# Denominators of a linear attention: chunk sums on VectorE, and an LN1 shared by two engines

## The chip, the cores and the metric

The kernel runs on one core of one Trainium2 chip. The metric is the device time of one execution in microseconds. Before the change it is 263.28 us, the median of three runs (262.45 to 264.20). A core has TensorE (PE, matmuls, with its weight loads listed as PEld), VectorE (DVE), ScalarE (ACT), GpSimd (POOL) and SyncE (SP). Each takes its instructions in the order of the program and waits for the others by semaphores. In this kernel nearly all DMAs are issued from SP's queue, which is in order as well: a DMA whose data isn't ready holds back every later one.

## The reference

```python
# x: 2048 x 640; H = 32 heads of 20; F = 1728; all bf16
g = sigmoid((x * gate_w).sum(-1, keepdims=True))

q, k, v = split(x @ wqkv)                 # (32, 2048, 20) each
phi = lambda t: where(t > 0, t + 1, exp(t)) + 1e-6
pq, pk = phi(q), phi(k)
kv  = einsum("bhsd,bhse->bhde", pk, v)
z   = einsum("bhsd->bhd", pk)             # sum of phi(k) over the rows
num = einsum("bhqd,bhde->bhqe", pq, kv)
den = einsum("bhqd,bhd->bhq", pq, z) + 1e-6
a = (num / den) @ wo

h  = gelu(layernorm(x) @ w1)              # LN1
hs = shift_rows_by_quarter(h) @ w2        # quarters of the columns moved by +1, -1, +2, -2 rows
x1 = x + hs
b  = x1 + gelu(layernorm(x1) @ w3) @ w4   # LN2
return g * a + (1 - g) * b
```

## The kernel before, in words

The 2048 rows are 16 chunks of 128 (`c`), in four tiles of 512 (`t`); `cc` is a chunk within its tile. The 640 columns are five blocks of 128 (`j`, `dc`, `fc`). The program order is written out by hand (`manual_schedule`), so the order of the source is the order of each engine's queue.

The stages, with the lines of the profile:

- **k** (L186): 16 chunks of phi(k) into `pk`, rows on partitions. **q** (L241): phi(q) into `pqT`, columns on partitions, so that `pqT[:, j, s]` holds block j of row s. `xT`, the transposed x, is read only up to here.
- **G** (`g_unit(j)`, L318): the product of phi(k) with x, five units of 32 matmuls, each about 4.4 us. x has a column of ones behind it, so column 320 of the second half of each PSUM result is z, the sum of phi(k), for the 128 columns of block j. ScalarE copies the rest to `gs` (L320), two buffers in turn, and SP transposes it into `gT` (L322). VectorE makes `zbd[:, j, :]` (L321), z spread over 32 heads by a mask, as bf16.
- **LN1**: `ln1_stat(c)` takes mean and variance on VectorE (L292 to L294), `ln1_rstd(t)` the reciprocal root for a tile's four chunks on GpSimd (L288, L289), `ln1_apply(c)` writes the normalised chunk on VectorE (L308) and SP transposes it into `lnxT` (L310). These run beside G.
- **w1** (`w1_unit(t, fcs)`, L352): three units for each tile, of two, two and one column blocks. ScalarE applies gelu (L356), and for the last unit writes `hx` (L359), which VectorE copies in four strips into `hsT` (L362).
- **kv** (`kv_unit`, L371): gT with the v weights; VectorE masks the result into `kvT` in three pieces (L377). Then `m_unit(g)` (L385), six units of two matmuls, multiplies with the output weights; ScalarE copies each result to `mst` (L387), `m_store` writes these to DRAM in three DMAs (L391) and `m_load` reads them back, arranged anew, as `m_sb` in six (L397).
- **Denominators**: `den_mm` (L256) multiplies all five blocks of `pqT` with `zbd`, 20 matmuls; the four row tiles go to the four 32-partition strips of one PSUM bank. `den_evac` (L262) adds 1e-6 on VectorE, `den_recip` (L267) takes the reciprocal, `r_spread` copies it to four tiles (L271) and four DMAs spread it over the partitions as `rb` (L273). `scale_t(t)` (L277) multiplies `pqT` of tile t by it.
- **w2** (`w2_unit(t, cc)`, L435) and the residual add into a float32 `x1` tile (L438), then LN2 (`ln2_rstd`, `ln2_apply`, with a transpose from SP at L454). Then for each tile t: **w3** (`w3_unit`, L485, gelu at L487), **att** (`att_unit`, L466, added at L472), **w4** (L524, L560), output.

PSUM results take turns in four pairs of banks (`pair()`): a unit can start only when the result four units earlier has been read out.

What matters for the order around the change: after `g_unit(4)` come `w1_unit(0, ...)` three times, `kv_unit`, `w1_unit(1, (0, 1))`, `den_mm`, three `m_unit`s, `w1_unit(1, (2, 3))`, two `m_unit`s, `w1_unit(1, (4,))`, the last `m_unit`, `m_store`, and `w2_unit(0, ...)`. VectorE does `den_evac`, four `ln1_apply` and `den_recip` in that stretch. `r_spread` follows the last `ln2_apply` of tile 0, and `m_load` follows all of `w1_unit(2, ...)`. In the loop over t, tile 0's w3 units alternate with `w2_unit(1, ...)`, from the first on.

Of the kernel before, what the change touches and what calls it, by code (L numbers as in the profile page):

```python
# [16 lines left out]
def kernel(  # L17
# [32 lines left out]
    NG = 6  # L50
# [11 lines left out]
    small = ctx.enter_context(tc.tile_pool(name="small", bufs=4))  # L62
    work = ctx.enter_context(tc.tile_pool(name="work", bufs=4))
    hx_p = ctx.enter_context(tc.tile_pool(name="hx_p", bufs=3))
    outp = ctx.enter_context(tc.tile_pool(name="outp", bufs=4))
    lnx_p = ctx.enter_context(tc.tile_pool(name="lnx_p", bufs=3))
    ps = ctx.enter_context(tc.tile_pool(name="ps", bufs=4, space=PSUM))
    dram = ctx.enter_context(tc.tile_pool(name="dram", bufs=1, space=bass.MemoryType.DRAM))
# [14 lines left out]
    m_sb = const.tile([P, DC, D], BF16)  # L83
    kvT = const.tile([P, D], BF16)
    rb = const.tile([P, NT, TS], BF16)
    r_bf = const.tile([P, TS], BF16)
    r4 = const.tile([H, NT, TS], BF16)
    ident = const.tile([P, P], BF16)
# [1 line left out]
    g5z = const.tile([P, P], BF16)  # L90
    mhalf = const.tile([P, CPT], F32)
    hmask = const.tile([P, H], F32)
    zbd = const.tile([P, DC, H], BF16)
    bmask = const.tile([P, GH * 4], F32)
    bmask5 = const.tile([P, 8], F32)
    ylog = const.tile([P, NCH], F32)
# [58 lines left out]
    for c in range(0, NCH, CPT):  # L155
# [89 lines left out]
    def gate_ops():  # L245
# [3 lines left out]
        nc.vector.reciprocal(omg[:], omg[:])  # L249
        nc.vector.tensor_tensor(gate[:], gate[:], omg[:], op=ALU.mult)  # L250

    def den_mm():
        pt = pair()
        for j in range(DC):
            for t in range(NT):
                nc.tensor.matmul(pt[32 * t:32 * (t + 1), 0, :], lhsT=zbd[:, j, :], rhs=pqT[:, j, t * TS:(t + 1) * TS],  # L256
                                 start=(j == 0), stop=(j == DC - 1))
        return pt

    def den_evac(pt):  # L260
        d = x1p.tile([P, D], F32, name="x1")[:, 0:TS]
        nc.vector.tensor_scalar_add(d, pt[:, 0, :], 1e-6)  # L262
        return d

    def den_recip(d):
        with nc.allow_low_precision(reason="rounded after a float32 division, as a copy would"):
            nc.vector.reciprocal(r_bf[:], d)  # L267
# [28 lines left out]
    def ln1_stat(c):  # L296
        ln_stats(mv1[:, c, :], x_sb[:, c, 0:D], st1s[:, c])

    def ln1_rstd(t):
        tt = slice(t * CPT, (t + 1) * CPT)  # L300
        rsqrt(rstd1[:, tt], mv1[:, tt, 1])

    def ln1_apply(c):
        t, cc = divmod(c, CPT)
        if cc == 0:
            lnxT[t] = lnx_p.tile([P, DC, TS], BF16, name="lnxT")
        lnx = work.tile([P, D], BF16, name="ln")
        nc.vector.tensor_scalar(lnx[:], x_sb[:, c, 0:D], mv1[:, c, 0:1], rstd1[:, c:c + 1],  # L308
                                op0=ALU.subtract, op1=ALU.mult)
        nc.sync.dma_start_transpose(lnxT[t][:, :, cc * P:(cc + 1) * P], lnx[:])  # L310


    def g_unit(j):
        pt = pair()
        for c in range(NCH):
            w = pk[:, c, :].rearrange("p (m j) -> p j m", j=DC)[:, j]
            for hf in range(2):
                nc.tensor.matmul(pt[:, hf, 0:HD + hf], lhsT=w, rhs=x_sb[:, c, hf * HD:(hf + 1) * HD + hf],  # L318
                                 start=(c == 0), stop=(c == NCH - 1))
        nc.scalar.copy(gs[:, j % 2, :].rearrange("p (h e) -> p h e", h=2), pt[:, :, 0:HD])  # L320
        nc.vector.tensor_scalar_mul(zbd[:, j, :], hmask[:], pt[:, 1, HD:HD + 1])  # L321
        nc.sync.dma_start_transpose(gT[:, :, j * P:(j + 1) * P], gs[:, j % 2, :])  # L322

    for c in range(CPT):
        ln1_stat(c)
    ln1_rstd(0)
    g_unit(0)
    for cc in range(CPT):
        ln1_stat(CPT + cc)
        ln1_apply(cc)  # L330
    ln1_rstd(1)
    g_unit(1)
    for cc in range(CPT):
        ln1_stat(2 * CPT + cc)
        ln1_apply(CPT + cc)
    ln1_rstd(2)
    g_unit(2)
    for cc in range(CPT):
        ln1_stat(3 * CPT + cc)
    ln1_rstd(3)  # L340
    g_unit(3)
    g_unit(4)
    for cc in range(CPT):
        ln1_apply(2 * CPT + cc)


# [35 lines left out]
    def m_unit(g):  # L382
        pt = pair()
        for hf in range(2):
            nc.tensor.matmul(pt[:, hf, 0:HD], lhsT=kvT[:, row0[g]:row0[g] + P],  # L385
                             rhs=wo_sb[:, g, hf * HD:(hf + 1) * HD], start=True, stop=True)
        nc.scalar.copy(mst[g // 2][:, g % 2, :].rearrange("p (h e) -> p h e", h=2), pt[:, :, 0:HD])  # L387

    def m_store():
        for i in range(NG // 2):  # L390
            nc.sync.dma_start(m_dram[2 * i:2 * i + 2].rearrange("g p e -> p g e"), mst[i])  # L391
# [9 lines left out]
    nc.gpsimd.memset(hsT[:, :, S:S + 4], 0.0)  # L401
    for fcs in w1_split:
        w1_unit(0, fcs)
    kv_unit()
    w1_unit(1, w1_split[0])
    s1.close()
    w4p = ctx.enter_context(tc.tile_pool(name="w4p", bufs=1))
    w4_sb = w4p.tile([P, FF + 1, D], BF16)
    h2x_p = ctx.enter_context(tc.tile_pool(name="h2x_p", bufs=2))
    h2p = ctx.enter_context(tc.tile_pool(name="h2p", bufs=1))  # L410
    x1p = ctx.enter_context(tc.tile_pool(name="x1p", bufs=11))
    den = den_evac(den_mm())
    mst = [x1p.tile([P, D], F32, name="x1")[:].bitcast(BF16).rearrange("p (g e) -> p g e", g=2) for _ in range(NG // 2)]
    for cc in range(CPT):
        ln1_apply(3 * CPT + cc)
    den_recip(den)
    for g in range(3):
        m_unit(g)
    w1_unit(1, w1_split[1])
    for g in range(3, 5):  # L420
        m_unit(g)
    w1_unit(1, w1_split[2])
    m_unit(5)
    m_store()
    st = {}


# [104 lines left out]

    def w4_turned_out(t, cc):
        c = t * CPT + cc
        oc = outp.tile([P, D], BF16, name="oc")
        o = t * TS + cc * P
        nc.vector.scalar_tensor_tensor(oc[:].rearrange("p (d f) -> p d f", d=DC), pqT[:, :, o:o + P], omg[:, c:c + 1],  # L537
                                       st[t]["x1"][cc][:].rearrange("p (d f) -> p d f", d=DC), op0=ALU.mult, op1=ALU.add)
        nc.sync.dma_start(out2[c * P:(c + 1) * P, :], oc[:])

    def w4_stt(t, cc, oc, src, a, b):
        c = t * CPT + cc
# [7 lines left out]
    def w4_last(t):  # L550
        pts, ocs = {}, {}

        def place(pairs, homes):
            for cc, (w, n) in homes.items():
                pts[cc, 0], pts[cc, 1] = (pairs[n][:, 1, 0:NW], 0, NW), (pairs[w][:, 0, :], NW, D)

        def mm(cc, hf, start):
            dst, a, b = pts[cc, hf]
            for fc in range(FF):
                nc.tensor.matmul(dst, lhsT=st[t]["h2"][:, fc * TS + cc * P:fc * TS + (cc + 1) * P],  # L560
                                 rhs=w4_sb[:, fc, a:b], start=start and fc == 0, stop=not start and fc == FF - 1)

        prs = [pair() for _ in range(3)]
        place(prs, {0: (0, 1), 2: (1, 2)})
        for cc in (0, 2):
            for hf in (1, 0):
                mm(cc, hf, True)
        prs.append(pair())
        place(prs, {1: (3, 3), 3: (2, 0)})
        for u in range(2):  # L570
            for hf in range(2):
                for v in range(2):
                    rows = slice(FR * v, FR * (v + 1))
                    dst, a, b = pts[u + 2 * v, hf]
                    cc = u + 2 * v
                    nc.tensor.matmul(dst, lhsT=st[t]["h2x"][rows, cc * P:(cc + 1) * P],
                                     rhs=w4_sb[rows, FF, a:b], start=u == 1, stop=u == 0)
        for cc in (0, 2):
            oc = outp.tile([P, D], BF16, name="oc")
            for hf in range(2):  # L580
                w4_stt(t, cc, oc, *pts[cc, hf])
            w4_store(t, cc, oc, 0, D)
        for cc, hf in ((1, 1), (3, 1), (1, 0), (3, 0)):
            mm(cc, hf, False)
            if hf == 1:
                ocs[cc] = outp.tile([P, D], BF16, name="oc")
            w4_stt(t, cc, ocs[cc], *pts[cc, hf])
            w4_store(t, cc, ocs[cc], *pts[cc, hf][1:])

    for cc in range(CPT):  # L590
        w2_unit(0, cc)
        ln2_rstd(0, cc, cc + 1)
        if cc >= 1:
            ln2_apply(0, cc - 1)
    for fcs in w1_split:
        w1_unit(2, fcs)
        if fcs[0] == 0:
            ln2_apply(0, CPT - 1)
            r_spread()
    m_load()  # L600
    nc.sync.dma_start(w4_sb[:, 0:FF, :], B_w4[0:FF * P, :].rearrange("(c p) f -> p c f", p=P))
    nc.sync.dma_start(w4_sb[0:FR, FF, :], B_w4[FF * P:F, :])
    nc.sync.dma_start(w4_sb[FR:P, FF, :], B_w4[FF * P:F, :])
# [57 lines left out]
```

## Time and profile before

| | us |
|---|---|
| median of three runs | 263.28 |
| profiled execution | 262.68 |
| its span, first to last instruction | 261.0 |
| TensorE busy in it | 256.0 |
| VectorE busy | 141.4 |
| ScalarE busy | 93.5 |

The profile page gives totals for each engine, the chain of work that ended last (followed back from the last instruction through whatever released each step), and groups of equal instructions with their mean duration. In a group line the name before the arrow is what is written, those behind it what is read; then the shape, the type, the count, the busy time, the mean in ns and the idle time in front of them with what ended it. Some of the groups around the change:

```profile
L256 PE MATMUL pp<-pqT,zbd 128*32 128x512 bf16 x20 | 1.3, 381 | 0.0
L321 DVE TENSOR_SCALAR zbd<-hmask,pp 128x32 bf16<-128x32 f32 x5 | 1.1, 224 | 1.3 <-ACT gs L320 1.3
L308 DVE TENSOR_SCALAR ln<-x_sb,mv,rstd 128x640 bf16<-128x640 bf16 x16 | 6.3, 424 | 0.4 <-POOL rstd L289 0.3
L320 ACT CAST gs<-pp 128x640 bf16<-128x640 f32 x5 | 3.5, 692 | 19.7 <-PE pp L318 14.4 <-DMA wk_sb<-gs 5.3
L267 DVE RECIPROCAL r_bf<-x 128x512 bf16<-128x512 f32 x1 | 3.3, 3348 | 0.0
```

A matmul's own duration (381 ns here) is longer than its share of the chain, since matmuls overlap in the array.

### The profile page before, as it was taken

What the parts mean: (1) busy time and instruction counts of PE and PEld (TensorE: products, weight loads), DVE (VectorE), ACT (ScalarE), POOL (GpSimd) and SP (SyncE); (2) the same over time, 40 slices, a digit from 0 to 9 for tenths busy, and PEclk for the clock granted to TensorE, in tenths of its full rate; (3) what the DMA queues carried; (4) which work ended last, traced back from release to release, by engine and by line L of the source; (5) the groups of instructions that cost most, each with busy time, mean ns of one, the idle gap of its engine ahead of it and who ended that gap; (6) DMA issues with size and microseconds to landing.
All of it is one profiled execution on the core that took longest, in us unless ns stands there. A gap on an engine that the chain in (4) does not pass through costs nothing.

```text
span 261.0 us, 4113 instructions
## 1 busy us (share of the span) xinstructions
PE 256.0 (98%) x1601; PEld 151.5 (58%) x1625; DVE 141.4 (54%) x276; ACT 93.5 (36%) x144; POOL 27.9 (11%) x82
## 2 busy tenths in 40 slices
PE   8999999999999999999999999999999999999995
PEld 4677555688854644566464566455565546465543
DVE  2688778799947894876300398600287610125132
ACT  1655454321165446532343322342322344342100
POOL 3000050012220140131000131000023000000000
PEclk9999999999999999999999999999999999999999
DMA  7999996016684836994032123312123402211011
GB/s 206 204 147 378 365 338 242 0 28 121 122 107 82 216 65 133 186 311 88 14 43 40 20 52 90 81 23 57 23 50 73 102 20 43 43 44 54 24 50 53
DMA packets 57558, 28.28 MB, mean 108 GB/s; under 512 B 45506, under 2 KB 56770, under 8 KB 57538
## 3 DMA queue, kind: packets, MB, share of 16 engines
q1 hardware_dynamic: 57096, 27.52, 44.1%
q10 hardware_dynamic: 442, 0.49, 0.5%
q8 instruction: 13, 0.21, 0.4%
q14 instruction: 7, 0.06, 0.1%
HBM read 13.03 MB, written 3.60 MB: 64 GB/s over the span
## 4 chain that ended last, share of the span: by engine, by line
PE 98%; issue 1%; DVE 0%
PE pp L485 21%; PE pp L524 16%; PE pp L186 9%; PE pp L318 8%; PE pp L435 8%; PE pp L466 8%; PE pp L241 8%; PE pp L352 8%; PE pp L560 5%; PE pp L199 1%; PE pp L495 1%; PE pp L516 1%; PE pp L385 1%; PE pp L371 1%; PE pp L256 0%
## 5 line engine op out<-in xcount | busy, mean ns | idle before, releaser
L485 PE MATMUL pp<-lnxT,w_sb 128*128 128x512 bf16 x249 | 59.8, 379 | 0.6
L487 ACT ACTIVATE h<-pp 128x1024 bf16<-128x1024 f32 (+1 forms) x28 | 26.9, 962 | 56.0 <-PE pp L485 56.0
L524 PE MATMUL pp<-h,w_sb 128*128 128x512 bf16 (+1 forms) x228 | 42.4, 343 | 0.3
L485 PEld LDWEIGHTS <-w_sb 128*128 128x128 bf16 x260 | 25.2, 98 | 26.9
L438 DVE TENSOR_TENSOR x<-pp,x_sb 128x640 f32<-128x640 f32 x16 | 13.1, 817 | 42.7 <-PE pp L435 42.7
L524 PEld LDWEIGHTS <-w_sb 128*128 128x128 bf16 x234 | 22.7, 98 | 19.5 <-issue 1.0
L178 ACT ACTIVATE e<-pp 128x640 bf16<-128x640 f32 (+1 forms) x26 | 21.5, 827 | 9.5 <-PE pp L241 9.5
L466 PE MATMUL pp<-m_sb,pqT 128*128 128x320 bf16 x160 | 24.3, 299 | 0.0
L472 DVE SCALAR_TENSOR_TENSOR x<-pp,gate,x 128x640 f32<-128x640 f32 x16 | 14.1, 883 | 18.3 <-PE pp L466 12.6
L435 PE MATMUL pp<-w_sb,hsT 128*128 128x320 bf16 x160 | 23.9, 299 | 0.0
L186 PE MATMUL pp<-wk_sb,xT 128*128 128x320 bf16 (+1 forms) x160 | 23.0, 303 | 0.1
L288 POOL TENSOR_SCALAR rstd<-mv 128x1 f32<-128x1 f32 (+1 forms) x20 | 7.7, 385 | 142.1 <-DVE mv L294 142.1
L318 PE MATMUL pp<-x_sb,pk 128*128 128x320 bf16 (+1 forms) x160 | 22.0, 300 | 0.0
L241 PE MATMUL pp<-xT,hsT 128*128 128x512 bf16 x98 | 21.6, 379 | 0.1
L318 PEld LDWEIGHTS <-pk 128*128 128x128 bf16 x160 | 18.8, 117 | 3.2
L435 PEld LDWEIGHTS <-hsT 128*128 128x128 bf16 x160 | 15.6, 98 | 8.0
L466 PEld LDWEIGHTS <-pqT 128*128 128x128 bf16 x160 | 15.7, 98 | 7.7
L537 DVE SCALAR_TENSOR_TENSOR oc<-pqT,omg,x 128x640 bf16<-128x640 bf16 x12 | 10.5, 877 | 16.8 <-DMA pqT<-hx 16.8
L186 PEld LDWEIGHTS <-xT 128*128 128x128 bf16 x160 | 15.6, 99 | 6.9 <-DVE xT L215 0.9
L352 PE MATMUL pp<-lnxT,w_sb 128*128 128x512 bf16 x77 | 17.9, 379 | 0.2
L241 PEld LDWEIGHTS <-hsT 128*128 128x128 bf16 x100 | 11.8, 118 | 9.7
L528 ACT CAST hx<-pp 128x512 bf16<-128x512 f32 x12 | 7.0, 586 | 22.5 <-PE pp L524 14.9
(80 smaller groups left out, 236.6 us busy)
## 6 DMA issues: line engine op xcount, KB each, us to landing
x_sb<-in_A_x_dram SPq DMA_DIRECT2D x1, 2240.0 KB
out_dram<-oc SPq DMA_DIRECT2D x14, 160.0 KB, 1.9
w_sb<-in_B_w_dram SPq DMA_DIRECT2D x1, 2160.0 KB, 11.0
w_sb<-in_B_w_dram SPq DMA_DIRECT2D x1, 2080.0 KB
wo_sb<-in_A_wo_dram SPq DMA_DIRECT2D x6, 160.0 KB, 7.9
m_dram<-x SPq DMA_DIRECT2D x3, 320.0 KB, 5.0
hsT<-in_A_wqkv_dram SPq DMA_DIRECT2D x1, 800.0 KB
m_sb<-in_A_wqkv_dram SPq DMA_DIRECT2D x1, 800.0 KB
```

The lines of the kernel that those rows point to most:

```text
L178: nc.scalar.activation(ev, src, ACT.Exp)
L186: nc.tensor.matmul(pt[:, hf, 0:n], lhsT=xT[:, dc, c * P:(c + 1) * P], rhs=wk_sb[:, dc, hf * HD:hf * HD + n], start=(dc == first), stop=(dc ...
L241: nc.tensor.matmul(pt[:, t % 2, :], lhsT=wq_sb[:, dc, :].rearrange("p (m j) -> p j m", j=DC)[:, j], rhs=xT[:, dc, t * TS:(t + 1) * TS], st ...
L318: nc.tensor.matmul(pt[:, hf, 0:HD + hf], lhsT=w, rhs=x_sb[:, c, hf * HD:(hf + 1) * HD + hf], start=(c == 0), stop=(c == NCH - 1))
L352: nc.tensor.matmul(pt[:, i, :], lhsT=w, rhs=lnxT[t][:, dc, :], start=(dc == 0), stop=(dc == DC - 1))
L435: nc.tensor.matmul(pt[:, hf, 0:HD], lhsT=hsT[:, fc, 2 + c * P:2 + (c + 1) * P], rhs=w2_sb[:, fc, hf * HD:(hf + 1) * HD], start=(fc == 0), ...
L438: nc.vector.tensor_tensor(x1[:].rearrange("p (h e) -> p h e", h=2), pt[:, :, 0:HD], x_sb[:, c, 0:D].rearrange("p (h e) -> p h e", h=2), op ...
L466: nc.tensor.matmul(pt[:, hf, 0:HD], lhsT=pqT[:, j, c * P:(c + 1) * P], rhs=m_sb[:, j, hf * HD:(hf + 1) * HD], start=(j == 0), stop=(j == D ...
L472: nc.vector.scalar_tensor_tensor(x1, pt[:, :, 0:HD], gate[:, c:c + 1], x1, op0=ALU.mult, op1=ALU.add)
L485: nc.tensor.matmul(pt[:, k, :], lhsT=w3_sb[:, dc, fc * P:(fc + 1) * P], rhs=lnT[:, dc, :], start=(dc == 0), stop=(dc == DC - 1))
L487: nc.scalar.activation(h2[:, 2 * i * TS:(2 * i + n) * TS], pt[:].rearrange("p h e -> p (h e)")[:, 0:n * TS], ACT.Gelu_apprx_tanh)
L524: nc.tensor.matmul(dst, lhsT=w4_sb[:, fc, d * P:(d + 1) * P], rhs=st[t]["h2"][:, fc * TS + a:fc * TS + b], start=False, stop=(fc == FF - 1))
```

## The change

z is no longer spread over heads. ScalarE copies it to a float32 `z[:, j]`. `den_add(j)` then sums the five blocks before any matmul: `u = sum over j of z_j * pqT_j`, 128 partitions by 2048 columns in float32, in two halves of 1024 columns. Block 0 is written by ScalarE, the other four are accumulated by VectorE. `u` lies in the memory of `xT`. `den_hi` copies u to bf16 on ScalarE, `den_lo` takes what that rounding lost, also as bf16, on VectorE, and `den_mm` multiplies both parts with the constant head mask: eight matmuls instead of 20.

LN1: of the 16 `ln1_apply`, 12 go to ScalarE (which needs `nmr1`, minus mean times rstd, a small VectorE product); chunks 10 to 13 stay on VectorE. Reciprocal roots of the first and last tile are taken in halves. The last tile's statistics are moved behind G, and its chunks 14 and 15 are applied after `den_evac`. As every gs transpose is issued from the same queue as the LN1 transposes, their order changes too: the last G transpose no longer stands behind as many of them.

In the stage after kv, `den_mm` moves behind the fifth `m_unit`; `den_recip` and `r_spread` move behind the last `ln2_apply` of tile 0, and `m_load` between that tile's first and second `ln2_apply`. The output tiles `oc4` are four fixed ones, and `mst` borrows them and `rb`.

```diff
+    mst = [oc4[:, 0:2, :], oc4[:, 2:4, :], rb[:].rearrange("p t s -> p (t s)")[:, 0:2 * D].rearrange("p (g e) -> p g e", g=2)]
...
-    zbd = const.tile([P, DC, H], BF16)
+    z = const.tile([P, DC], F32)
+    hm_bf = const.tile([P, H], BF16)
...
+    nc.gpsimd.tensor_copy(hm_bf[:], hmask[:])
...
+    halves = (slice(0, S // 2), slice(S // 2, S))
+    u = xT[:, 0:2, :].bitcast(F32).rearrange("p a s -> p (a s)")
+
+    def den_add(j):
+        for sl in halves:
+            if j == 0:
+                nc.scalar.activation(u[:, sl], pqT[:, j, sl], ACT.Copy, scale=z[:, j:j + 1])
+            else:
+                nc.vector.scalar_tensor_tensor(u[:, sl], pqT[:, j, sl], z[:, j:j + 1], u[:, sl], op0=ALU.mult, op1=ALU.add)
+
+    def den_hi(sl):
+        nc.scalar.copy(xT[:, 4, sl], u[:, sl])
+
+    def den_lo(sl):
+        nc.vector.tensor_tensor(xT[:, 3, sl], u[:, sl], xT[:, 4, sl], op=ALU.subtract)
+
     def den_mm():
         pt = pair()
-        for j in range(DC):
+        for n in range(2):
             for t in range(NT):
-                nc.tensor.matmul(pt[32 * t:32 * (t + 1), 0, :], lhsT=zbd[:, j, :], rhs=pqT[:, j, t * TS:(t + 1) * TS],
-                                 start=(j == 0), stop=(j == DC - 1))
+                nc.tensor.matmul(pt[32 * t:32 * (t + 1), 0, :], lhsT=hm_bf[:], rhs=xT[:, 4 - n, t * TS:(t + 1) * TS],
+                                 start=(n == 0), stop=(n == 1))
         return pt
...
+    def ln1_nmr(t, a=0, b=CPT):
+        tt = slice(t * CPT + a, t * CPT + b)
+        nc.vector.scalar_tensor_tensor(nmr1[:, tt], mv1[:, tt, 0], -1.0, rstd1[:, tt], op0=ALU.mult, op1=ALU.mult)
...
+        if eng is nc.scalar:
+            nc.scalar.activation(lnx[:], x_sb[:, c, 0:D], ACT.Identity, bias=nmr1[:, c:c + 1], scale=rstd1[:, c:c + 1])
...
+        nc.scalar.copy(z[:, j:j + 1], pt[:, 1, HD:HD + 1])
         nc.scalar.copy(gs[:, j % 2, :].rearrange("p (h e) -> p h e", h=2), pt[:, :, 0:HD])
-        nc.vector.tensor_scalar_mul(zbd[:, j, :], hmask[:], pt[:, 1, HD:HD + 1])
```

The order beside and behind G in the new kernel (loops written short):

```python
ln1_stat(0..3), rstd after 1 and after 3;  ln1_nmr(0, 0, 2)
g_unit(0);  den_add(0);  ln1_apply(0, 1) on ScalarE
g_unit(1);  ln1_stat(4..7), ln1_nmr(0, 2, 4) after 5;  ln1_rstd(1);  ln1_apply(2, 3) on ScalarE;  den_add(1)
g_unit(2);  ln1_stat(8..11), ln1_nmr(1) after 8;  ln1_rstd(2);  ln1_apply(4..7) on ScalarE
g_unit(3);  den_add(2);  den_add(3);  ln1_nmr(2)
g_unit(4);  den_add(4);  ln1_apply(8, 9) on ScalarE;  ln1_stat(12, 13);  ln1_rstd(3, 0, 2);  ln1_apply(10, 11)
w1_unit(0, ...) x3;  den_hi x2;  kv_unit;  den_lo x2
ln1_stat(14, 15);  ln1_rstd(3, 2, 4);  ln1_apply(12, 13);  w1_unit(1, (0, 1))
m_unit(0), (1);  w1_unit(1, (2, 3));  m_unit(2), (3);  w1_unit(1, (4,));  m_unit(4);  den_mm;  m_unit(5);  m_store
den_evac;  ln1_nmr(3, 2, 4);  ln1_apply(14, 15) on ScalarE
w2_unit(0, 0..3) with ln2_rstd and ln2_apply(0, cc - 1);  m_load after ln2_apply(0, 0)
w1_unit(2, (0, 1));  ln2_apply(0, 3);  den_recip;  r_spread;  w1_unit(2, (2, 3)), (4,)
```

More of the change, by code (lines that the diff above doesn't have):

```diff
@@ L64 @@
     hx_p = ctx.enter_context(tc.tile_pool(name="hx_p", bufs=3))
-    outp = ctx.enter_context(tc.tile_pool(name="outp", bufs=4))
     lnx_p = ctx.enter_context(tc.tile_pool(name="lnx_p", bufs=3))
@@ L85 @@
     rb = const.tile([P, NT, TS], BF16)
+    oc4 = const.tile([P, CPT, D], BF16)
+    mst = [oc4[:, 0:2, :], oc4[:, 2:4, :], rb[:].rearrange("p t s -> p (t s)")[:, 0:2 * D].rearrange("p (g e) -> p g e", g=2)]
     r_bf = const.tile([P, TS], BF16)
@@ L101 @@
     rstd1 = const.tile([P, NCH], F32)
+    nmr1 = const.tile([P, NCH], F32)
     wq_sb = hsT[:, :, 0:D]
@@ L297, in ln1_stat, with ln1_rstd, ln1_apply @@
         ln_stats(mv1[:, c, :], x_sb[:, c, 0:D], st1s[:, c])
-    def ln1_rstd(t):
-        tt = slice(t * CPT, (t + 1) * CPT)
+    def ln1_rstd(t, a=0, b=CPT):
+        tt = slice(t * CPT + a, t * CPT + b)
         rsqrt(rstd1[:, tt], mv1[:, tt, 1])
-    def ln1_apply(c):
+    def ln1_nmr(t, a=0, b=CPT):
+        tt = slice(t * CPT + a, t * CPT + b)
+        nc.vector.scalar_tensor_tensor(nmr1[:, tt], mv1[:, tt, 0], -1.0, rstd1[:, tt], op0=ALU.mult, op1=ALU.mult)
+    def ln1_apply(c, eng=nc.vector):
         t, cc = divmod(c, CPT)
@@ L307, in ln1_apply @@
         lnx = work.tile([P, D], BF16, name="ln")
-        nc.vector.tensor_scalar(lnx[:], x_sb[:, c, 0:D], mv1[:, c, 0:1], rstd1[:, c:c + 1],
-                                op0=ALU.subtract, op1=ALU.mult)
+        if eng is nc.scalar:
+            nc.scalar.activation(lnx[:], x_sb[:, c, 0:D], ACT.Identity, bias=nmr1[:, c:c + 1], scale=rstd1[:, c:c + 1])
+        else:
+            nc.vector.tensor_scalar(lnx[:], x_sb[:, c, 0:D], mv1[:, c, 0:1], rstd1[:, c:c + 1],
+                                    op0=ALU.subtract, op1=ALU.mult)
         nc.sync.dma_start_transpose(lnxT[t][:, :, cc * P:(cc + 1) * P], lnx[:])
@@ L325 @@
         ln1_stat(c)
-    ln1_rstd(0)
+        if c % 2 == 1:
+            ln1_rstd(0, c - 1, c + 1)
+    ln1_nmr(0, 0, 2)
     g_unit(0)
+    den_add(0)
+    for cc in range(2):
+        ln1_apply(cc, nc.scalar)
+    g_unit(1)
     for cc in range(CPT):
         ln1_stat(CPT + cc)
-        ln1_apply(cc)
+        if cc == 1:
+            ln1_nmr(0, 2, CPT)
     ln1_rstd(1)
-    g_unit(1)
+    for cc in range(2, CPT):
+        ln1_apply(cc, nc.scalar)
+    den_add(1)
+    g_unit(2)
     for cc in range(CPT):
         ln1_stat(2 * CPT + cc)
-        ln1_apply(CPT + cc)
+        if cc == 0:
+            ln1_nmr(1)
     ln1_rstd(2)
-    g_unit(2)
     for cc in range(CPT):
+        ln1_apply(CPT + cc, nc.scalar)
+    g_unit(3)
+    den_add(2)
+    den_add(3)
+    ln1_nmr(2)
+    g_unit(4)
+    den_add(4)
+    for cc in range(2):
+        ln1_apply(2 * CPT + cc, nc.scalar)
+    for cc in range(2):
         ln1_stat(3 * CPT + cc)
[L340 to L343, printed above, removed]
+    ln1_rstd(3, 0, 2)
+    for cc in range(2, CPT):
         ln1_apply(2 * CPT + cc)
@@ L403 @@
         w1_unit(0, fcs)
+    for sl in halves:
+        den_hi(sl)
     kv_unit()
-    w1_unit(1, w1_split[0])
+    for sl in halves:
+        den_lo(sl)
+    for cc in range(2, CPT):
+        ln1_stat(3 * CPT + cc)
+    ln1_rstd(3, 2, CPT)
+    for cc in range(2):
+        ln1_apply(3 * CPT + cc)
+    w1_unit(1, w1_split[0])
+    for g in range(2):
+        m_unit(g)
+    w1_unit(1, w1_split[1])
+    for g in range(2, 4):
+        m_unit(g)
+    w1_unit(1, w1_split[2])
+    m_unit(4)
+    den_ps = den_mm()
+    m_unit(5)
+    m_store()
     s1.close()
@@ L411 @@
     x1p = ctx.enter_context(tc.tile_pool(name="x1p", bufs=11))
[L412 to L424, printed above, removed]
+    den = den_evac(den_ps)
+    ln1_nmr(3, 2, CPT)
+    for cc in range(2, CPT):
+        ln1_apply(3 * CPT + cc, nc.scalar)
     st = {}
@@ L534, in w4_turned_out @@
         c = t * CPT + cc
-        oc = outp.tile([P, D], BF16, name="oc")
+        oc = oc4[:, cc, :]
         o = t * TS + cc * P
-        nc.vector.scalar_tensor_tensor(oc[:].rearrange("p (d f) -> p d f", d=DC), pqT[:, :, o:o + P], omg[:, c:c + 1],
+        nc.vector.scalar_tensor_tensor(oc.rearrange("p (d f) -> p d f", d=DC), pqT[:, :, o:o + P], omg[:, c:c + 1],
                                        st[t]["x1"][cc][:].rearrange("p (d f) -> p d f", d=DC), op0=ALU.mult, op1=ALU.add)
-        nc.sync.dma_start(out2[c * P:(c + 1) * P, :], oc[:])
+        nc.sync.dma_start(out2[c * P:(c + 1) * P, :], oc)
     def w4_stt(t, cc, oc, src, a, b):
@@ L578, in w4_last @@
         for cc in (0, 2):
-            oc = outp.tile([P, D], BF16, name="oc")
+            oc = oc4[:, cc, :]
             for hf in range(2):
@@ L585, in w4_last @@
             if hf == 1:
-                ocs[cc] = outp.tile([P, D], BF16, name="oc")
+                ocs[cc] = oc4[:, cc, :]
             w4_stt(t, cc, ocs[cc], *pts[cc, hf])
@@ L594 @@
             ln2_apply(0, cc - 1)
-    for fcs in w1_split:
+        if cc == 1:
+            m_load()
+    w1_unit(2, w1_split[0])
+    ln2_apply(0, CPT - 1)
+    den_recip(den)
+    r_spread()
+    for fcs in w1_split[1:]:
         w1_unit(2, fcs)
[L597 to L600, printed above, removed]
     nc.sync.dma_start(w4_sb[:, 0:FF, :], B_w4[0:FF * P, :].rearrange("(c p) f -> p c f", p=P))
```

## The prediction

> **What bounds the kernel now.** I read the page first, then the chain of work that ended last in order of time between 73 and 92 us, then the timeline of the same stretch, then the waits.
>
> ```profile
> span 261.0 us, 4113 instructions
> PE 256.0 (98%) x1601; PEld 151.5 (58%) x1625; DVE 141.4 (54%) x276; ACT 93.5 (36%) x144; POOL 27.9 (11%) x82
> PE 98%; issue 1%; DVE 0%
> ```
>
> Engine totals and the chain's shares, from the page. TensorE is busy 256 of 261 us and carries the chain; the tables of its waits hold 0.8 us at the start and 0.2 us at the end, none between. So only fewer TensorE slots, or a new TensorE stall, can move the time.
>
> ```profile
> 80.00 1.19 PE pp L256 x20
> 81.20 0.92 PE pp L385 x6
> 82.12 2.19 PE pp L352 x10
> 84.31 0.54 PE pp L385 x4
> ...
> 85.93 0.27 PE pp L385 x2
> 86.20 5.46 PE pp L435 x40
> ```
>
> The chain (start, length, line). L256 is the old denominator product: 1.19 us of chain for 20 matmuls, 0.06 each. One 128x512 matmul of L352 takes 0.219, so the four that write different 32-row strips run side by side.
>
> ```profile
> 84.35 1.09 ACT L356 ACTIVATE hsT<-pp 128x512 bf16<-128x512 f32 x2 [0.81 <-PE pp L352]
> ...
> 85.32 1.29 ACT L387 CAST x<-pp 128x640 bf16<-128x640 f32 x2
> ...
> 86.48 0.64 ACT L359 ACTIVATE hx<-pp 128x512 bf16<-128x512 f32 x1
> ...
> 98.77 1.16 DVE L271 COPY r<-r_bf 32x512 bf16<-32x512 bf16 x4
> ...
> 105.30 1.49 DVE L277 TENSOR_TENSOR pqT<-pqT,rb 128x2560 bf16<-128x2560 bf16 x1 [4.14 <-DMA m_sb<-m_dram]
> ```
>
> The timeline. From starts to next starts ScalarE needs 0.97 for a gelu pair and 1.16 for two casts. L277 starts 5.37 us after the copies of L271 end at 99.93, and VectorE was idle 4.14 us before it: that idle time is the cover the change uses up.
>
> **TensorE: the gain.** Twenty matmuls become eight. In proportion: 1.19 x 8/20 = 0.48, a gain of 0.71 us. Five sets of four at 0.219 make 1.09 of the 1.19, so up to 0.10 may be paid once per visit; then eight cost 0.54 and the gain is 0.65. I take 0.71, with 0.65 as the other end.
> The Trainium skill, "TensorEngine Tiling (Array Packing)", Key Properties, says that a change of tiling mode drains the array: a rule against a product this short, placed between two full-array ones. The chain shows 81.20 after 80.00 + 1.19; by the rule the whole 0.10 is drain and the gain 0.65, by the row taken in proportion 0.71.
>
> **VectorE until the masks of kvT (L377).** The five zbd multiplications (L321, 0.224 each) and most LN1 applications (L308, 0.424) leave; eight accumulations over 1024 columns come in. No row shows that form. The same operation with a pointer scalar and a float32 second source takes 883 ns for 640 columns (L472), 746 for 512 and 348 for 128 (L543): slope 1.036 ns, hence 0.883 + 384 x 0.001036 = 1.28 us. Neighbours overlap by about 0.08 (L438 starts 0.08 before the L294 ahead of it ends), so 1.20. Bounds: 0.44 (L179, 1024 bf16, one source) and 1.41 (0.883 x 1.6). From 51.97: 14 statistics at 1.00 (four fill 51.97 to 55.98), four small products at 0.19 (L250 0.174), 8 x 1.20, two applications at 0.38: 51.97 + 14.0 + 0.76 + 9.6 + 0.76 = 77.1. Next in its queue are the four L362 copies, which need ScalarE's hx.
> ScalarE to there: g_unit(4) ends at 71.00; z copy 0.16 (L190), gs 0.69, to 71.9; the third small product (VectorE, 51.97 + 12 + 0.57 + 7.2 = 71.7) is there; two applications at 0.83 (L459, 640 columns, pointer scale; bounds 0.70 of L178 and 0.92) end at 73.5; table load 1.28 to 74.8, against 74.69 before. The gelus follow 0.1 late, hx ends at 77.35, the copies at 78.55, the first mask (0.53) at 79.1. m_unit(0), which now follows w1_unit(1) at once, wants it at 80.00 instead of 81.20. Margin 0.9: no stall. The cover is gone when an accumulation exceeds 1.20 + (0.25 + 0.9)/8 = 1.34 us.
> The Trainium skill, "ScalarE: Activation LUTs", What ACT_TABLE_LOAD costs, has each per-partition pointer operand add about 93 ns; the new application has two, so 0.92 by an estimate from it, and 0.09 more for each in front of the table load, still inside that margin.
>
> **Edits that cost nothing on the path.** The last G transpose: gs waited 5.27 us for a transpose and went out at 73.40 in front of kv at 76.40; now it goes at about 72, so kv's slack grows by 1.4 and hides it. hm_bf is one 0.2 us GpSimd copy in an idle queue. Halved rstd calls finish under VectorE's statistics. den_hi: 1024 columns at 1.02 (L178) to 1.14 (plus the 0.12 by which L459 exceeds L178), two end at 79.5, before the gelus of w1_unit(1) at 80.04: 0.5 of cover. den_lo: two at 1.22 (L180's 1024 columns) after the masks (79.5) end at 82, against den_mm at 84.7: 2.7 of cover. The buffers that replace outp and three x1 tiles are recycled as before.
>
> **First new wait: w2_unit(0,0).** Four PSUM pairs rotate. With den_mm late, w2_unit(0,0) gets the pair of w1_unit(1,(4,)), no longer m_unit(3)'s, so it waits for hx. w1_unit(1,(2,3)) ends at 80.00 + 0.61 + 2.19 = 82.80. ScalarE: 82.84 + 0.97 + 1.16 + 0.64 = 85.61, and 0.06 to pass the word. TensorE is ready at 86.20 - 0.71 = 85.49. Stall 0.18, bounds 0 and 0.4 (m5 waits likewise for m3's cast at 85.1, wanted at 85.2).
>
> **Second new wait: w2_unit(1,2).** The reciprocal (L267, 3.35) moves behind the last LN2 application. VectorE: hx copies to 86.85, denominators 0.69, a small product, first residual add 87.65 against 88.37, so this queue is 0.72 early and the last application ends at 98.13 (98.85 before). Reciprocal and copies: 98.13 + 3.35 + 1.16 - 0.1 = 102.55; + 5.37 gives scale_t(0) at 107.9, 2.6 later than 105.30. Behind it in the queue stand the four hx copies of w1_unit(3) (1.19) and the add of w2_unit(1,0): 107.9 + 1.49 - 0.08 + 1.19 + 0.82 + 0.06 = 111.36. w2_unit(1,2) needs that pair at 111.64 - 0.71 + 0.18 = 111.11. Stall 0.25; bounds 0 (rb lands sooner with m_load's 800 KB out of its way) and 0.8. What is late after it, the pairs of w3_unit(0,3) and (0,4), keeps over 1 us.
>
> **SP's queue.** m_load (2.64 us of issue) stands in front of three LN2 transposes and waits for the stores. Stores go out at 87.5 (before 87.61) and land 5.0 later, 92.5; transposes of t=3 to 91.6, the first LN2 transpose to 93.25, m_load to 95.9, the others at 95.9, 97.1 and 98.3, each 1.2. The last lands 2.6 later, at 100.9; w3_unit(0,0) wants it at 102.45 - 0.53 = 101.92. Cover 1.0.
>
> **Sum.** -0.71 + 0.18 + 0.25 = -0.28 us. The profiled execution (262.68, of which 1.68 lies outside the span) would become 262.40; the median of the runs shown, 263.28, is 0.60 above it, so 263.0.
>
> **Rivals.**
> *Nothing stalls.* ScalarE or rb is a few tenths quicker than I put it; both stalls are smaller than 0.3, which speaks for it. 263.28 - 0.71 = 262.6.
> *Slower: m_load blocks SP.* If the stores land late, m_load holds the LN2 transposes and w3_unit(0,0) stalls. It decides once the last transpose cannot be issued by 99.3, that is m_load not by 94.26, or stores landing over 6.8 us after issue; from 7.1 the kernel is slower than before. For it: wo_sb's 160 KB took 7.9 and transposes crowd the same 16 DMA engines (75% busy from 86 to 92). Against: this same store in almost the same place took 5.0. At 7.9 the stall is 1.1 and the time 264.1; at the 12.0 that w4's remainder took, 268.2.
> *VectorE holds m_unit(0).* Accumulations at 1.41: 8 x 0.07 = 0.6, time 263.6; against it two row forms that agree on 1.28 before overlap.
> *The product doesn't shrink,* the eight running one after another: 8 x 0.219 = 1.75, +0.56 instead of -0.71, 264.3. The old 20 in 1.19 with the same strips speak against it.
>
> **How the numbers follow.** Forecast 0.60, no stall 0.17, SP 0.10, VectorE 0.08, product or something unforeseen 0.05. The three runs before spread from 262.45 to 264.2, so a median of few runs moves by some 0.5. Low end: 262.6 less 0.4 = 262.2. High end: SP at 7.9 plus 0.6 = 264.7, which leaves out about 0.12 in all. The forecast's own range is 262.4 to 263.7. What a measurement can tell is 1%, or 2.6 us. Faster by that is beyond the whole gain: 0.02. Slower needs the stores at over 9.7 us or a stall I do not see: 0.07. Within 1%: 0.91.
>
> **What would show it.** Right: the denominator's chain piece at about 0.5 us with eight matmuls; the chain at w2_unit(0,0) and w2_unit(1,2) with a few tenths of waiting for ScalarE and VectorE; accumulations at 1.2 to 1.3; VectorE's idle time before scale_t(0) still near 4 us, but starting near 107.9. Wrong: a TensorE wait in front of m_unit(0) (masks), of w1_unit(1) (gelus behind den_hi), or of w3_unit(0,0) (SP), or accumulations beyond 1.34.

## The result, and the profile after

| | before | after |
|---|---|---|
| median (us) | 262.87 (262.45 to 264.20, 6 runs) | 267.0 (265.17 to 269.32, 6 runs) |
| ratio after / before | | 1.0137, 95% interval 1.0094 to 1.0180 |
| profiled execution | 262.68 | 269.32 |
| its span | 261.0 | 267.6 |

The ratio leaves out the profiled execution, 269.32, as a disturbed run; what disturbed it turns out below to belong to the change. The three runs of the kernel before that are given above are among its six here. The kernel is slower, by 0.9 to 1.8%; 263.0 was predicted, with a range from 262.2 to 264.7.

The page of the new kernel: span, totals of the engines, the chain's shares, and some groups around the change.

```profile
span 267.6 us, 4153 instructions
PE 258.4 (97%) x1613; PEld 151.5 (57%) x1613; DVE 148.8 (56%) x274; ACT 107.3 (40%) x165; POOL 32.2 (12%) x87
PE 76%; DVE 14%; DMA 3%; ACT 3%; issue 2%; POOL 1%; SPq 0%; DVEq 0%; POOLq 0%
...
L264 DVE SCALAR_TENSOR_TENSOR xT<-pqT,z,xT 128x1024 f32<-128x1024 bf16 x8 | 9.8, 1271 | 0.1
L333 ACT ACTIVATE ln<-x_sb,nmr,rstd 128x640 bf16<-128x640 bf16 x12 | 10.3, 914 | 1.9 <-issue 1.0 <-DVE nmr L325 0.8
```

TensorE is busy 2.4 us longer although it does less (1.8 of it is a lower clock, below), and the chain, 98% TensorE before, leaves it for a quarter of the span. VectorE leads the shares of the rest, but a share says who stood in the chain, not what stalled. That is in the table of TensorE's waits (line waited for: total us, times, longest):

```profile
PE pp L540 <- DMA lnxT<-ln: 2.8, 1, 2.8
PE pp L190 <- DMA wk_sb<-in_A_wqkv_dram: 1.1, 2, 0.8
PE pp L430 <- ACT xT L267: 1.0, 1, 1.0
...
PE pp L397 <- ACT hsT L401: 0.7, 1, 0.7
```

L540 (w3), L430 (`m_unit`) and L397 (w1) wait in the middle of the kernel, where nothing waited before. L190 is the start: the k matmuls wait for their first loads, which differs from one execution to the next (it isn't in the next profile of the same kernel).

**First place: the gelus.** The timeline from 76 to 83 us (start, length, engine, line; in brackets the idle time before and its releaser):

```profile
76.58 0.32 POOL L308 TENSOR_SCALAR rstd<-mv 128x2 f32<-128x2 f32 x1 [6.08 <-DVE mv L314]
76.98 0.76 POOL L309 TENSOR_TENSOR rstd<-rstd,mhalf 128x2 f32<-128x2 f32 x1
77.70 0.11 POOL L445 MEMSET hsT<- 128x20 bf16 x1
...
77.84 2.06 ACT L401 ACTIVATE hsT<-pp 128x512 bf16<-128x512 f32 x4 [2.66 <-POOL hsT L445]
78.98 2.32 PE L397 MATMUL pp<-lnxT,w_sb 128*128 128x512 bf16 x10 [0.74 <-ACT hsT L401]
...
82.31 0.72 PE L430 MATMUL pp<-wo_sb,kvT 128*128 128x320 bf16 x4 [1.01 <-ACT xT L267]
```

Read upward: TensorE waits for a gelu to free its pair, the gelu waited 2.66 us for a memset of `hsT`'s edge columns on GpSimd, the memset stands behind `ln1_rstd` of chunks 12 and 13, and that waits for their statistics on VectorE, which end at 76.5 because VectorE has the new accumulations first. Before, the memsets ran at 73.36, ahead of the gelu at 74.69. `m_unit(0)` (L430) is late for the same reason: `hx`, its copies and the masks of `kvT` follow these gelus in turn, and its weight load waited 1.50 us for the first mask. The releaser named for its matmul, ScalarE's L267, ended at about the same time.

**Second place: w3_unit(0,0).** SP's timeline, then the chain of waits there:

```profile
91.65 3.16 SPq L337 DMA_TRANSPOSE lnxT<-ln  x2
94.92 2.89 SPq L509 DMA_TRANSPOSE lnxT<-ln  x1
98.31 2.37 SPq L442 DMA_DIRECT2D m_sb<-m_dram  x6
100.78 4.34 SPq L509 DMA_TRANSPOSE lnxT<-ln  x3
```

```profile
103.44 3.67 DMA lnxT<-ln
107.11 0.14 issue
107.25 3.99 PE pp L540 x10
```

`m_load` (L442) goes out 8.3 us after the first store (89.97), the last of the LN2 transposes behind it (L509) at 103.44, and this one takes 3.67 us to land; in the kernel before, all four landed 2.6 us after they were issued. It isn't the stores that hold `m_load`: by the trace's semaphore records they landed 2.5 to 3.6 us after issue, the last at 94.75. `m_load` stands behind the first LN2 transpose, which takes 2.89 us to issue instead of 1.21 and is itself behind two LN1 transposes (L337). TensorE was done with w1 at 104.4, hence the 2.8 us. Then its ten matmuls take 3.99 us instead of 2.16. Two stretches of the table by window say why (window, its length, busy us of PE, PEld, DVE, ACT and POOL, granted TensorE clock, DMA share, GB/s):

```profile
106.00:108.00 2.00, 0.76 (x2) 0.29 (x3) 0.61 (x3) 1.99 (x3) 0.00 (x0) 0.81 0.90 174
108.00:112.00 4.00, 4.00 (x16) 1.82 (x15) 1.69 (x2) 0.73 (x1) 0.00 (x0) 0.67 0.92 245
```

The granted clock falls to 0.67 after the wait.

The 6.6 us of span of this one execution, from the starts of the same units in both traces: 0.45 at the start; 1.5 up to w2_unit(0,0), where 0.74 and 1.01 of waiting and some 0.4 of restarts and smaller waits stand against 0.64 saved on the denominators; 2.8 of waiting at w3_unit(0,0); 1.8 of lower clock behind it.

### The profile page after: what moved, and what is told of

It is laid out like the page before. It is cut to its first block, busy times and chain, and to the rows that moved or that the text cites. A ratio compares the mean times of both kernels' runs of the same rounds, so it can differ in the third digit from the quotient of the medians.

```text
span 267.6 us, 4153 instructions
## 1 busy us (share of the span) xinstructions
PE 258.4 (97%) x1613; PEld 151.5 (57%) x1613; DVE 148.8 (56%) x274; ACT 107.3 (40%) x165; POOL 32.2 (12%) x87
## 4 chain that ended last, share of the span: by engine, by line
PE 76%; DVE 14%; DMA 3%; ACT 3%; issue 2%; POOL 1%; SPq 0%; DVEq 0%; POOLq 0%
PE pp L540 22%; PE pp L579 16%; PE pp L521 8%; PE pp L245 8%; PE pp L190 8%; PE pp L490 6%; PE pp L615 5%; DVE xT L264 3%; DVE st1s L313 2%; DVE st1s L312 2%; DMA wk_sb<-in_A_wqkv_dram 2%; DMA lnxT<-ln 1%; DVE mv L314 1%; ACT hsT L401 1%; DVE x L493 1%
## 5 line engine op out<-in xcount | busy, mean ns | idle before, releaser
L540 PE MATMUL pp<-lnxT,w_sb 128*128 128x512 bf16 x260 | 62.0, 387 | 2.8 <-DMA lnxT<-ln 2.8
L540 PEld LDWEIGHTS <-w_sb 128*128 128x128 bf16 x260 | 25.5, 99 | 31.2 <-issue 5.5
L308 POOL TENSOR_SCALAR rstd<-mv 128x1 f32<-128x1 f32 (+2 forms) x22 | 8.9, 403 | 144.0 <-DVE mv L314 143.1
L190 PE MATMUL pp<-wk_sb,xT 128*128 128x320 bf16 (+1 forms) x160 | 22.4, 299 | 1.1 <-DMA wk_sb<-in_A_wqkv_dram 1.1
L190 PEld LDWEIGHTS <-xT 128*128 128x128 bf16 x160 | 15.6, 98 | 7.6 <-issue 1.1
L397 PE MATMUL pp<-lnxT,w_sb 128*128 128x512 bf16 x80 | 18.1, 379 | 0.7 <-ACT hsT L401 0.7
L309 POOL TENSOR_TENSOR rstd<-rstd,mhalf 128x1 f32<-128x1 f32 (+2 forms) x22 | 17.2, 782 | 1.8
```

What stands on the lines that cost most here:

```text
L190: nc.tensor.matmul(pt[:, hf, 0:n], lhsT=xT[:, dc, c * P:(c + 1) * P], rhs=wk_sb[:, dc, hf * HD:hf * HD + n], start=(dc == first), stop=(dc ...
L309: nc.gpsimd.tensor_tensor(out_ap, out_ap, mhalf[:, 0:out_ap.shape[1]], op=ALU.pow)
L397: nc.tensor.matmul(pt[:, i, :], lhsT=w, rhs=lnxT[t][:, dc, :], start=(dc == 0), stop=(dc == DC - 1))
L540: nc.tensor.matmul(pt[:, k, :], lhsT=w3_sb[:, dc, fc * P:(fc + 1) * P], rhs=lnT[:, dc, :], start=(dc == 0), stop=(dc == DC - 1))
```

## The experiments

Two theories: the memsets in GpSimd's queue and `m_load` in SP's, against rivals that need neither (VectorE simply has too much work by 78 us; the denominator product costs more than it saves; the transposes are late for some other reason). The first four kernels undo either, both or nothing, and ran together on one chip; so did the next four.

**a1: the changed kernel, unchanged**

> The changed kernel as it is, for a second profile: in the first, ten matmuls of w3_unit(0,0) took 3.99 us at a granted clock of 0.67 after a 2.8 us stall, where 2.16 is normal. Theory (two queues): the stalls recur, gelus held by GpSimd's memsets (about 1.7 us of TensorE) and w3_unit(0,0) held by the LN2 transposes behind m_load (2 to 3 us); 266.5 us. If the clock dip belongs to the change, it recurs too; if the run was disturbed, it does not.

267.87 us against 262.70, ratio 1.0176 (1.0131 to 1.0220). Its profile has the same stalls in the table of TensorE's waits, those at L430 (1.0) and L397 (0.7) in the same size, the third in another:

```profile
PE pp L540 <- DMA lnxT<-ln: 2.1, 1, 2.1
```

and in its windows:

```profile
104.00:106.00 2.00, 0.30 (x2) 0.21 (x3) 1.75 (x7) 2.00 (x4) 0.00 (x0) 1.00 0.76 148
106.00:110.00 4.00, 4.00 (x15) 1.69 (x14) 0.61 (x1) 2.03 (x3) 0.00 (x0) 0.60 0.75 178
```

So both stalls and the drop of the clock belong to the kernel: its second profile has them again. The lower clock again costs 1.8: ten matmuls of w3 take 3.41 and the ten of w2 behind them 1.95, against 2.16 and 1.36 at full clock.

**a2: the memsets ahead of LN1's first statistics**

```diff
+    nc.gpsimd.memset(hsT[:, :, 0:4], 0.0)
+    nc.gpsimd.memset(hsT[:, :, S:S + 4], 0.0)
     for c in range(CPT):
         ln1_stat(c)
...
-    nc.gpsimd.memset(hsT[:, :, 0:4], 0.0)
-    nc.gpsimd.memset(hsT[:, :, S:S + 4], 0.0)
     for fcs in w1_split:
         w1_unit(0, fcs)
```

> The two memsets of hsT's edge columns stand ahead of LN1's first statistics instead of behind ln1_rstd(3,0,2) in GpSimd's queue. Theory (two queues): the first gelu starts near 75.2 instead of 77.8, TensorE's waits before w1_unit(1) and m_unit(0) go, 1.7 us or more are won against the changed kernel as it is (264.6). Rival (VectorE's backlog): the masks of kvT are late by the accumulations, and m_unit(0) still starts at 82; 266.5.

263.88 us, ratio 1.0047 (1.0031 to 1.0064). The first gelu starts at 74.70, and the waits at L397 and L430 are gone, with VectorE's work untouched: the rival of a VectorE that has too much to do falls. Of TensorE's waits in mid-kernel one is left, and the clock stays at 1.00 behind it:

```profile
PE pp L540 <- ACT x L514: 1.4, 1, 1.4
```

The releaser named is ScalarE's L514, which writes nothing that these matmuls read. They read the transposed tile; its last three transposes landed 5.1, 4.3 and 3.5 us after issue (the 3.5 by the trace's semaphore records), the last at 103.13, 0.14 us before these matmuls start. c1 below tests it.

**a3: `m_load` behind the last LN2 transpose of tile 0**

```diff
-        if cc == 1:
-            m_load()
     w1_unit(2, w1_split[0])
     ln2_apply(0, CPT - 1)
+    m_load()
     den_recip(den)
```

> m_load is moved back behind tile 0's last ln2_apply, ahead of the reciprocal; nothing else. Theory (two queues): the three transposes go out as their data come, w3_unit(0,0) does not wait, 2.8 us are won (263.7). Rival (traffic): the transposes are late because the stores' data fill the DMA engines, and the stall stays above 1.5 us; 265.5 or more.

264.25 us, ratio 1.0058 (1.0039 to 1.0077). The wait at L540 is gone, those at L397 (0.7) and L430 (1.0) stay. The stores are where they were, and the last transpose lands 2.6 us after issue, so the rival of the stores' data falls.

**a4: both**

> Both moves. Theory (two queues): both stalls go; what is left is the eight matmuls' gain of 0.65 to 0.71 less 0.2 at w2_unit(0,0) and 0.3 at w2_unit(1,2): 0.2 to 0.5 us under the kernel before. Rival (VectorE's backlog or traffic): a stall of over 1 us is left in the stretch from 71 to 107 us.

262.27 us, ratio 0.9980 (0.9967 to 0.9992). The table of TensorE's waits has none left in the middle of the kernel. This version beats the kernel before, by 0.2% (0.1 to 0.3%), and the changed one by 1.9% (0.9980 / 1.0176). The chain, from the last w1 units of tile 1 to the first w3 unit:

```profile
84.40 0.55 PE pp L276 x8
...
85.36 5.59 PE pp L490 x40
90.95 10.79 PE pp L399 x50
101.75 2.16 PE pp L540 x10
```

It is TensorE alone, with the new denominators at 0.55 us (L276). In spans, undoing the memsets alone is worth 266.1 - 261.9 = 4.2 us, `m_load` alone 266.1 - 262.2 = 3.9, both 266.1 - 260.3 = 5.8. That doesn't add up to 8.1 because each one alone already ends the drop of the clock: with both edits in, 1.7 + 2.1 + 1.8 = 5.6 of waits and clock are gone, while each one alone takes the 1.8 and its own share. That share is 1.7 and 0.7 for the memsets (the wait at w3_unit(0,0) is 1.4 in a2, not 2.1) and 2.1 for `m_load`.

**b1: the kernel before, with `m_load` moved alone**

```diff
         if cc >= 1:
             ln2_apply(0, cc - 1)
+        if cc == 1:
+            m_load()
...
-    m_load()
```

> The kernel before with one change: m_load stands between tile 0's first and second ln2_apply. Theory (SP's queue): it costs here too, without any of the other parts: the stores go out at 87.6, m_load holds the three transposes until about 97, and w3_unit(0,0) at 102.4 waits 0.5 to 1.5 us; 263.2 to 264.2 against 262.7. Rival (the position hurts only because the new kernel's stores are late): no wait, 262.7.

263.73 us against 262.48, ratio 1.0045 (1.0031 to 1.0060). TensorE waits 1.1 us at w3_unit(0,0), and the clock holds:

```profile
PE pp L485 <- DMA lnxT<-ln: 1.1, 1, 1.1
```

The move of `m_load` costs this much without any other part of the change; that part of the theory needs nothing else.

**b2: a4 with the old denominators**

```diff
-        for n in range(2):
+        for j in range(DC):
             for t in range(NT):
-                nc.tensor.matmul(..., lhsT=hm_bf[:], rhs=xT[:, 4 - n, t * TS:(t + 1) * TS],
+                nc.tensor.matmul(..., lhsT=zbd[:, j, :], rhs=pqT[:, j, t * TS:(t + 1) * TS],
```

(with the `zbd` multiplications back, and `den_add`, `den_hi` and `den_lo` out)

> As a4_both, but with the old denominators: zbd on VectorE and 20 matmuls at the new place; no z copy, accumulation or split. Theory (TensorE's term): 0.65 to 0.7 us slower than a4_both, so 262.9, the denominator's piece of the chain 1.19 instead of 0.55. Rival (the gain of a4_both comes from the LN1 and queue moves): 262.3, as a4_both.

262.58 us, ratio 0.9998 (0.9989 to 1.0007). Its chain at the same place:

```profile
84.59 1.19 PE pp L258 x20
85.78 0.38 PE pp L409 x2
86.16 5.43 PE pp L463 x40
```

1.19 against 0.55: the new product saves 0.64 us of chain. The two ratios differ by 0.0018, or 0.5 us; they are from different chips and their intervals overlap, so the trace is the better witness of the two.

**b3: a4 with all of LN1 on VectorE**

```diff
-        ln1_apply(cc, nc.scalar)
+        ln1_apply(cc)
```

(all 12 calls, and `ln1_nmr` out)

> As a4_both, but all 16 LN1 applications on VectorE, without the small products. Theory (VectorE has no room for both): ten applications of 0.38 in front of the masks make them about 2.5 us late, m_unit(0) waits some 1.5 us, 263.8. Rival (VectorE's backlog does not matter): 262.3.

264.14 us, ratio 1.0066 (1.0041 to 1.0092). Here VectorE is late, at the place that the prediction's rival named, though by LN1's applications and not by slower accumulations (1.28 each). TensorE's wait:

```profile
PE pp L412 <- ACT hx L400: 1.2, 1, 1.2
```

The releaser named is ScalarE's `hx`, but the chain of waits runs through VectorE's statistics, its copies of `hx` and its masks up to 81.2 us, 1.4 us after a4's first `m_unit` (79.80). VectorE has no room for the accumulations and all of LN1; moving LN1 to ScalarE is what makes room.

**b4: a2 with `m_load` issued from ScalarE**

```diff
-            nc.sync.dma_start(m_sb[4 * head0[g]:4 * head0[g] + n, :, :],
+            nc.scalar.dma_start(m_sb[4 * head0[g]:4 * head0[g] + n, :, :],
...
     w1_unit(2, w1_split[0])
+    m_load()
```

> As a2_memset, but the six loads of m_load are issued from ScalarE's queue, behind the first gelus of w1_unit(2), at about the same time (94.3 to 97). Theory (SP's queue: what is queued behind the loads is late): the transposes go out as their data come, the wait of w3_unit(0,0) (1.4 us in a2_memset) is under 0.3, 262.4. Rival (traffic: the loads' data hold the transposes' data in the DMA engines): the wait stays at 1 us or more, 263.5 or more.

266.10 us, ratio 1.0108 (1.0075 to 1.0141): a miss. The transposes went out as soon as their data was ready, but the loads held ScalarE itself. Its timeline:

```profile
94.05 7.77 ACTq L444 DMA_DIRECT2D m_sb<-m_dram  x4
...
101.87 1.08 ACT L403 ACTIVATE hsT<-pp 128x512 bf16<-128x512 f32 x2 [7.75 <-DMA lnxT<-ln]
103.00 1.83 PE L399 MATMUL pp<-lnxT,w1x 128*128 128x512 bf16 x5 [2.46 <-ACT hsT L403]
```

The four loads stretch over 7.77 us, though each takes 0.5 us or less to issue: by the trace's semaphore records the second and the third of them went out 0.02 us after a transpose of SP had landed whose DMA semaphore they wait for. ScalarE stood idle for 7.75 us before the gelu behind them, TensorE waited 2.46 us, and the clock dropped to 0.50 (104 to 106 us). So the wait at w3_unit(0,0), on which the expectation rests, can't be read here. The landing of the LN2 transposes can:

```profile
DMA to landing us min/median/max: 4.0/5.2/6.5
```

The view tells of two of the four; by the semaphore records the last three took 6.5, 4.7 and 4.0 us, where a4's took 2.6 to 2.7. No load stood in front of them in SP's queue, so this speaks for the traffic.

**c1: a2 with a fifth of `m_load`'s data**

```diff
-            nc.sync.dma_start(m_sb[... + n, :, :],
-                              m_dram[...].rearrange("(j r) e -> r j e", j=DC))
+            nc.sync.dma_start(m_sb[... + n, 0:1, :],
+                              m_dram[...].rearrange("(j r) e -> r j e", j=DC)[:, 0:1, :])
```

> As a2_memset, with m_load at its new place, but each of its six DMAs loads one of the five blocks of m_sb (the other four keep what was there, so the attention part is computed from wrong data); same number of DMA instructions in SP's queue, a fifth of the data. a2_memset waited 1.4 us: its last transpose went out 1.6 late and landed in about 3.5 instead of 2.6. If the queue order alone makes the wait, it stays at 1.0 or more; if the loads' data in the DMA engines do, it goes below 0.5, and each transpose lands in 2.6 to 3 us.

262.95 us against 262.62, ratio 1.0006 (0.9987 to 1.0025). SP's timeline of a2, then of c1:

```profile
94.28 2.56 SPq L444 DMA_DIRECT2D m_sb<-m_dram  x6
96.95 4.01 SPq L509 DMA_TRANSPOSE lnxT<-ln  x3
```

```profile
94.64 2.29 SPq L444 DMA_DIRECT2D m_sb<-m_dram  x6
97.04 3.88 SPq L509 DMA_TRANSPOSE lnxT<-ln  x3
```

The same six DMAs in the same place, and three transposes that go out at the same time; but they land later in a2 (first) than in c1:

```profile
DMA to landing us min/median/max: 4.3/4.7/5.1
```

```profile
DMA to landing us min/median/max: 2.6/2.6/2.6
```

The first view doesn't tell of a2's last transpose, which took 3.5. The wait at w3_unit(0,0) falls from 1.4 to 0.2 us. Of the 1.2 that are gone, 0.9 is the landing of the last transpose (3.5 against 2.6). The other 0.3 is its issue, measured against TensorE, which is 0.4 us later in c1 at this point: the smaller loads take 2.29 us to issue instead of 2.56. So 1.2 of a2's 1.4 us come from the loads' 800 KB, most of it by traffic in front of the transposes, and 0.2 is left to the place of the six DMAs in the queue. The place by itself uses up the slack; the traffic turns the rest into a wait.

## Why the prediction was wrong, step by step

**Wrong: "Halved rstd calls finish under VectorE's statistics" and "The gelus follow 0.1 late".** This was costed at nothing, with no look at what stands behind these calls in GpSimd's queue: the two memsets that the first gelu needs. The gelu ran at 77.84 instead of 74.8, and TensorE waited 0.74 and 1.01. The prediction's sum for VectorE was near the truth, but it followed VectorE and ScalarE to the masks and left out the queue between them. a2 shows it.

**Wrong: "SP's queue", "Cover 1.0".** The sum had the last transpose issued at 98.3 and landed at 100.9, and TensorE ready for it at 101.92. a2, where the memsets are out of the way, is that case: issued at 99.6, landed at 103.13, TensorE ready at 101.85. Both terms were too small, the issue by 1.3 us and the landing by 0.9. In the issue, the first LN2 transpose was through at 93.79 instead of 93.25 (1.93 us for it instead of 1.2), `m_load` started another 0.5 us behind it (so in b1, a1, a2 and after), and the rest is in the transposes. The landing, 2.6 us, was taken from a stretch where no loads lay in front of them. The rival "m_load blocks SP" (0.10) named the place, but made it hang on stores that land late, over 6.8 us after issue. They landed sooner than the 5.0 that was taken: after 2.5 to 3.4 us in a2, 2.5 to 3.6 in after. `m_load` was at the rival's threshold of 94.26 in b1 (94.18) and a2 (94.28), where it allows no wait worth naming, and TensorE waited 1.1 and 1.4.

**Not in the sum: the clock.** A wait was priced at its length. The one at w3_unit(0,0) cost 1.8 us more behind it in both profiles. It isn't needed for the sign: runs without the drop took 265.2 to 267.6, slower too.

**The denominators: right, at the small end.** 0.65 or 0.71 was predicted, 0.71 taken; b2 and a4 give 0.64. The rule of the Trainium skill that was weighed there (the drain at a change of tiling mode, "TensorEngine Tiling (Array Packing)", Key Properties) agrees with the two chain pieces: 0.55 - 2 x 0.219 = 0.11 with two sets of four, 1.19 - 5 x 0.219 = 0.10 with five, so it is paid for each visit and not for each set. "The product doesn't shrink" is out.

**VectorE: right.** 1.28 us was worked out for an accumulation from rows of another shape, and 1.27 is measured (L264). The margin of 0.9 at `m_unit(0)` held: once the memsets are out of the way (a2, a4), no mask is late, and b3 shows how it looks when one is. ScalarE's LN1 takes 0.914 (L333), not the 0.83 that was taken; the estimate of 0.92 from the Trainium skill ("ScalarE: Activation LUTs", What ACT_TABLE_LOAD costs) was the better one, and the margin covered it, as was said.

**First new wait, w2_unit(0,0): right.** 0.18 predicted; in a4 it is 0.20: w2's 40 matmuls stand 0.04 behind the last `m_unit` and take 5.59 us of chain, in b2, where `hx` is ready in time, nothing behind it and 5.43. (The `m_unit` behind `den_mm` takes 0.38 instead of 0.27 in both; that is no wait.)

**Second new wait, w2_unit(1,2): wrong in its pair.** 0.25 was predicted (the sum behind it gives 111.38, not 111.36) and there is none. In a4:

```profile
110.78 1.52 PE L490 MATMUL pp<-w_sb,hsT 128*128 128x320 bf16 x10
...
111.66 0.82 DVE L493 TENSOR_TENSOR x<-pp,x_sb 128x640 f32<-128x640 f32 x1
```

`scale_t(0)` was even later than predicted (109.03 against 107.9), and the add behind it starts at 111.66, yet w2_unit(1,2) starts at 110.78. So it doesn't use the pair that this add frees: the count of four pairs in strict turn doesn't hold there. Which pair it uses wasn't traced.

With these, the prediction without its two queue errors would have been 262.68 - 0.64 + 0.20 = 262.2 for the profiled execution; a4's is 262.29.

## What to carry to other kernels

When an edit delays one instruction, write down everything that stands behind it in its own in-order queue, small set-up work such as a memset included, and who waits for each: both stalls here were of this kind, on the queues of GpSimd, 12% busy in the totals, and of SP, which they don't list. A DMA that moves ahead of others costs them twice, its place in the queue and its bytes in the engines; take a landing time from a stretch with the same traffic. Price a long TensorE wait above its length: those of 2.1 and 2.8 us here cost 1.8 more.

## What the runs showed of the hardware

**The clock.** What TensorE had waited, in one piece, and the granted clock in the windows behind it:

| run | wait (us) | clock behind it |
|---|---|---|
| b1 | 1.1 | no drop (mean 1.00) |
| b3 | 1.2 | no drop (mean 1.00) |
| a2 | 1.4 | 1.00 |
| a1 | 2.1 | 0.60 over 4 us |
| b4 | 2.5 | 0.50 over 2 us, 0.88 on both sides |
| after | 2.8 | 0.81 over 2 us, then 0.67 over 4 us |

The Trainium skill ("TensorE: Matmul & The Clock Gate", Why this matters for your kernels) says to keep idle gaps under about 3 us. Here 2.1 was enough. It doesn't strike in every execution: of ten runs of the changed kernel, the four with a mean clock of 0.994 took 267.8 to 269.3 us, the six at 0.999 or above 265.2 to 267.6. Where between 1.4 and 2.1 it begins, and what decides in the single run, stays open. So does what spreads the six by 2.4 us: both profiles of this kernel are of runs with the drop.

**GpSimd beside VectorE.** The reciprocal root of four chunks takes 1.05 us on GpSimd in b2, and 1.90 in the changed kernel, where VectorE's accumulations run beside it. The group in after, then in b2:

```profile
L309 POOL TENSOR_TENSOR rstd<-rstd,mhalf 128x4 f32<-128x4 f32 x2 | 3.8, 1895 | 0.2
```

```profile
L291 POOL TENSOR_TENSOR rstd<-rstd,mhalf 128x4 f32<-128x4 f32 x2 | 2.1, 1054 | 0.2
```

The Trainium skill ("SBUF — State Buffer", Who interferes with whom) has a VectorE instruction with two inputs in SBUF contend with a GpSimd instruction that reads SBUF, the later one blocked; the accumulations have two. In after the root starts 0.30 us into an accumulation and takes longer, as the rule has it. b3 agrees only in part:

```profile
60.91 1.07 POOL L309 TENSOR_TENSOR rstd<-rstd,mhalf 128x4 f32<-128x4 f32 x1
61.01 2.48 DVE L264 SCALAR_TENSOR_TENSOR xT<-pqT,z,xT 128x1024 f32<-128x1024 bf16 x2
```

Here the root starts first and isn't slowed, but the two accumulations beside it take 2.48 us, as in after, so the later one isn't seen to be blocked. No experiment isolates it, and no wait hangs on it here.
